# Sliding-block softmax by chained multiply-adds and ScalarE copies, with the buffers of the last chunks reassigned, in a two-part decode attention kernel

## Chip, cores, metric

One core of a Trainium2 chip. The metric is the time of one execution in device microseconds (us), median of several runs; lower is better. All runs told here are marked "fast" in the record: none lies more than 1.5% above the fastest of its kernel.

## The reference, cut to what matters

Two decode attentions over the same kind of cache, one query row per batch (4 batches), 32 query heads, head size 128; their outputs stand side by side.

```python
# A: 8 key heads, each for 4 query heads; only the last W = 2048 positions of 8192 ("sliding block")
scores = einsum("bhqd,bhkd->bhqk", q, k[:, :, Sk - W:]) * Dh ** -0.5
o_A = einsum("bhqk,bhkd->bhqd", softmax(scores), v[:, :, Sk - W:])   # then @ wo
# B: 32 key heads, all 8192 positions
o_B = einsum("bhqk,bhkd->bhqd", softmax(einsum("bhqd,bhkd->bhqk", q, k) * Dh ** -0.5), v)
out = concatenate([o_A @ wo_A, o_B @ wo_B], -1)
```

All inputs are bf16. The keys and values alone are 34 MB for A and 537 MB for B, each read once.

## The kernel before

The work is cut into 72 chunks: 0 to 7 are A (one key head, all four batches, 2 MB of keys and 2 MB of values), 8 to 71 are B (two heads of one batch, 4 MB and 4 MB). For each chunk PE transposes the keys (`tr`), VectorE or ScalarE copies them out of PSUM (`kt`), PE multiplies them with the queries (`sc`), the softmax follows, and one chunk later PE multiplies the probabilities (`pba` in A, `pbb` in B) with the values (`po`). All loads go through one queue, in program order, into ten buffers of 2 MB; each load waits for the last reader of its buffers.

In A a tile of 128 rows holds all four batches, so every score tile has 16 columns (4 batches x 4 heads), of which a row needs the four of its own batch. The kernel before multiplies with a mask and adds up, half a chunk at a time; GpSimd spreads the probabilities again to 16 columns.

```python
# buffers: at = first buffer of a load, take() returns what its last user must have done
at = HALF_A[kind][c % 5] if ch["ab"] == 0 else (0 if kind == "k" else 4) + 2 * (c % 2)
if kind == "v" and c == NC - 1:
    at = 8
waits = take((kind, c), at, 1 if ch["ab"] == 0 else 2, ("T", ch["s_last"]) if kind == "k" else ("pv", c))
...                                             # load order: k0 k1 v0 k2 v1 ... k69 v68 k70 k71 v69 v70 v71
def scores_out(c, half):                        # A only, twice per chunk
    dve.tensor_tensor(out=sel, in0=sc[:, half, :], in1=mk (broadcast), op=mult)      # 128x512
    dve.tensor_reduce(out=sA[half], in_=sel (b innermost), op=add)                   # 128x128
...                                             # stats_exp(c), A branch
    act.activation(ev, sA[:, c % 2, :], Exp)                                         # 128x256
    pool.tensor_tensor(out=pba, in0=ev (broadcast over b), in1=mkb (broadcast), op=mult)   # 128x1024
    dve.tensor_reduce(out=rs4, in_=ev, op=add)
    dve.tensor_tensor(out=rst, in0=rs4 (broadcast), in1=mk, op=mult)                 # 128x16
...                                             # end of the program
values_part(69, 71); values_only(70); emit_fin(69); emit_wos(71); norm_sum(71); values_only(71); emit_fin(71)
```

(The calls are shortened; the order and the operands are the kernel's.)

## Time and profile before

| | kernel before |
|---|---|
| time, median of 6 runs (lowest to highest) | 1388.06 us (1386.57 to 1389.91) |
| profiled run: span | 1384.0 us |
| DMA loads, share of 16 engines | 99.4% |
| busy PE, DVE (VectorE), ACT (ScalarE), POOL (GpSimd) | 1168.8, 672.5, 422.9, 19.2 us |
| mean granted clock of PE (share of full speed) | 0.932 |

PE's busy time is that of pipelined matmuls and says little by itself; the row to read first is that of the DMA engines. A transfer here is split over 16 DMA engines, each of which adds one to the semaphore when its share is in. The trace keeps the times of these 16 increments. "First" and "last landing" below are the first and the sixteenth.

### The profile page before, as it was taken

The page shows a single profiled execution, that of the slowest core. Times are in us where ns is not written, and L with a number is a line of the kernel's source. Part 1 is how long each engine was busy: PE and PEld are TensorE (multiplying, and loading weights), DVE is VectorE, ACT ScalarE, POOL GpSimd, SP SyncE. Part 2 cuts the span into 40 slices and gives each one's busy share as a digit, 9 for nine tenths or more (in the row PEclk, how much of TensorE's full clock was granted, in tenths as well). Part 3 has the DMA queues.
Part 4 walks back from the last instruction along what each step waited for, and adds up shares of the span by engine and source line. Part 5 has one row for each costly group of instructions (what it writes and reads, how often), then busy time and mean ns, then how long its engine had stood idle before and what let it go on. Part 6 is the DMA issues. An engine that isn't in the chain of part 4 may idle for free.

```text
span 1384.0 us, 57015 instructions
## 1 busy us (share of the span) xinstructions
PE 1168.8 (84%) x26768; PEld 1125.1 (81%) x26768; DVE 672.5 (49%) x1327; ACT 422.9 (31%) x617; POOL 19.2 (1%) x22
## 2 busy tenths in 40 slices
PE   4878868998889888888898889888888798888988
PEld 4767868897889788888888888887888788878887
DVE  2877534554445444444454444444444354444443
ACT  1333323332233223332233223322332233223332
POOL 1111000000000000000000000000000000000000
PEclk9999989999999899999999999999999999999998
DMA  9999999999999999999999999999999999999997
GB/s 398 416 416 423 425 428 421 417 428 434 430 433 430 428 431 434 429 428 432 430 434 430 429 431 433 431 427 432 429 435 429 431 430 433 431 429 430 430 409 319
DMA packets 29992, 588.02 MB, mean 425 GB/s; under 512 B 2656, under 2 KB 10864, under 8 KB 11120
## 3 DMA queue, kind: packets, MB, share of 16 engines
q1 hardware_dynamic: 29912, 587.22, 99.4%
q8 instruction: 40, 0.66, 0.2%
q14 instruction: 16, 0.13, 0.0%
q10 hardware_dynamic: 24, 0.01, 0.0%
HBM read 587.21 MB, written 0.01 MB: 424 GB/s over the span
## 4 chain that ended last, share of the span: by engine, by line
DMA 58%; PE 35%; DVE 5%; issue 2%; ACT 0%; SPq 0%; DVEq 0%
DMA kv<-in_B_k_cache_dram 55%; PE tr L322 21%; PE sc L324 9%; PE po L324 3%; DMA kv<-in_A_k_cache_dram 2%; DVE kt L385 1%; DVE sA L434 1%; DVE rsa L502 1%; PE ms L324 1%; DVE sel L427 1%; DVE rm L444 0%; DVE sA L491 0%; DVE rs L500 0%; ACT eA L494 0%; PE fin L324 0%
## 5 line engine op out<-in xcount | busy, mean ns | idle before, releaser
L322 PE MATMUL tr<-identb,kv 128*128 128x128 bf16 x8704 | 700.0, 231 | 159.6 <-DMA kv<-in_B_k_cache_dram 147.7
L385 DVE COPY kt<-tr 128x1024 bf16<-128x1024 bf16 x736 | 502.4, 690 | 468.8 <-PE tr L322 464.3
L322 PEld LDWEIGHTS tr<-identb,kv 128*128 128x128 bf16 x8704 | 555.7, 104 | 186.5 <-issue 98.2
L383 ACT ACTIVATE kt<-tr 128x1024 bf16<-128x1024 bf16 x352 | 360.2, 1023 | 646.4 <-PE tr L322 643.7
L324 PE MATMUL sc<-qb,kt 128*128 128x64 bf16 x8192 | 421.3, 196 | 2.5 <-DVE kt L385 2.2
L324 PEld LDWEIGHTS sc<-qb,kt 128*128 128x128 bf16 x8192 | 347.9, 100 | 5.4 <-DVE kt L385 2.6
L324 PE MATMUL po<-pbb,kv 128*128 128x64 bf16 (+1 forms) x8192 | 291.8, 192 | 14.9 <-issue 14.6
L324 PEld LDWEIGHTS po<-pbb,kv 128*128 128x128 bf16 x8192 | 264.5, 97 | 15.1 <-issue 12.9
L483 ACT ACTIVATE pbb<-sc,negb 64x128 bf16<-64x128 f32 x128 | 51.1, 399 | 296.4 <-DVE negb L473 288.5
L449 DVE TENSOR_REDUCE rm<-sc 64x1 f32<-64x128 f32 x128 | 37.0, 289 | 93.5 <-PE sc L324 92.6
L324 PE MATMUL sc<-qs,kt 128*128 128x64 bf16 (+3 forms) x512 | 25.9, 195 | 17.0 <-DVE kt L385 17.0
L473 DVE COPY negb<-ms 128x1 f32<-128x1 f32 (+1 forms) x72 | 11.4, 158 | 57.6 <-PE ms L324 57.6
L324 PEld LDWEIGHTS sc<-qs,kt 128*128 128x128 bf16 x512 | 20.7, 100 | 20.3 <-DVE kt L385 20.3
L461 DVE TENSOR_REDUCE gm<-ms 1x2 f32<-1x128 f32 (+1 forms) x72 | 20.1, 279 | 31.1 <-PE ms L322 30.8
L324 PE MATMUL ms<-identf,gx 1*128 1x1 f32 (+1 forms) x144 | 27.4, 257 | 0.6 <-DVE gx L465 0.6
L324 PEld LDWEIGHTS ms<-identf,gx 1*128 1x128 f32 (+1 forms) x144 | 21.3, 184 | 4.8 <-DVE gx L465 0.8
L483 ACT ACTIVATION_READ_ACCUMULATOR pbb<-sc,negb 64x1 f32 x128 | 23.7, 185 | 0.0
L324 PE MATMUL fin<-wos,oz 128*4 128x512 bf16 x64 | 20.1, 396 | 0.3 <-DVE oz L543 0.3
L322 PE MATMUL ms<-identf,rm 128*1 128x128 f32 (+1 forms) x72 | 19.6, 273 | 0.2 <-DVE rm L449 0.2
L324 PE MATMUL po<-pba,kv 128*128 128x64 bf16 x512 | 18.8, 193 | 0.0
L434 DVE TENSOR_REDUCE sA<-sel 128x128 f32<-128x512 f32 x16 | 17.0, 1063 | 0.5
L465 DVE TENSOR_SCALAR gx<-gm 1x128 f32<-1x128 f32 (+1 forms) x72 | 16.0, 222 | 2.5
(46 smaller groups left out, 179.8 us busy)
## 6 DMA issues: line engine op xcount, KB each, us to landing
kv<-in_B_k_cache_dram SPq DMA_DIRECT2D x64, 4096.0 KB, 26.9
kv<-in_B_v_cache_dram SPq DMA_DIRECT2D x63, 4096.0 KB, 31.5
kv<-in_A_k_cache_dram SPq DMA_DIRECT2D x8, 2048.0 KB, 27.6
kv<-in_A_v_cache_dram SPq DMA_DIRECT2D x8, 2048.0 KB, 26.5
kv<-in_A_wq_dram SPq DMA_DIRECT2D x1, 4096.0 KB, 12.6
kv<-in_B_wq_dram SPq DMA_DIRECT2D x1, 4096.0 KB, 27.7
wor<-in_A_wo_dram SPq DMA_DIRECT2D x8, 512.0 KB, 22.9
wor<-in_B_wo_dram SPq DMA_DIRECT2D x8, 512.0 KB, 32.4
```

The lines of the kernel that those rows point to most:

```text
L322: emit = lambda e: e.transpose(o, l, r)
L324: emit = lambda e: e.matmul(o, l, r, start=start, stop=stop)
L383: sch.add("act", lambda e: e.activation(dst, src, ACTF.Copy), waits=waits, key=("ev", s))
L385: sch.add("dve", lambda e: e.tensor_copy(dst, src), waits=waits, key=("ev", s))
L427: sch.add("dve", lambda e: e.tensor_tensor(out=sel[:, :].rearrange("p (j b c) -> p j b c", b=NB, c=REP), in0=sc[:, half, :].rearrange("p ( ...
L434: sch.add("dve", lambda e: e.tensor_reduce(out=dst, in_=sel[:, :].rearrange("p (j b c) -> p j c b", b=NB, c=REP), axis=AX.X, op=ALU.add), ...
L449: sch.add("dve", lambda e, src=src, pp=pp: e.tensor_reduce(out=rm[pp, m, 0:1], in_=src, axis=AX.X, op=ALU.max), waits=[("S", ch["s_last"]) ...
L461: sch.add("dve", lambda e: e.tensor_reduce(out=gm[0:C, m, 0:U], in_=src, axis=AX.X, op=ALU.max), waits=[("trm", c)], key=("gmax", c))
L465: sch.add("dve", lambda e: e.tensor_scalar(out=dst, in0=gv, scalar1=-scale, scalar2=None, op0=ALU.mult), waits=[("gmax", c)], key=("gx", c))
L473: sch.add("dve", lambda e: e.tensor_copy(negb[:, m, 0:C], ms[:, col:col + C]), waits=[("bc", c)], key=("negb", c))
L483: sch.add("act", lambda e, src=src, pp=pp, n=n, u=u: e.activation(pbv[pp, :, u], src, ACTF.Exp, bias=negb[pp, m, 0:1], scale=scale, accum_ ...
L502: sch.add("dve", lambda e: e.tensor_tensor(out=rst[0][:, m, :].rearrange("p (b c) -> p b c", b=NB), in0=bcast(rs4[:, m, :], [[0, NB], [1, ...
```

## The change

Its intent: in A, take the own-batch scores straight from PSUM by four chained operations with the mask column as a scalar, without a mask product and a reduction; let ScalarE write the probabilities, so that GpSimd is idle (a small VectorE product beside its product takes 1514 ns); at the end, use buffers that come free sooner, so that the keys of 70 and 71 and the values of 69 are issued earlier; and put small work of the end between matmuls.

```diff
-            if kind == "v" and c == NC - 1:
-                at = 8
+            at = {("k", NC - 2): 8, ("k", NC - 1): 0, ("v", NC - 1): 2}.get((kind, c), at)
...
-        def scores_out(c, half):
-            ... mask product over 512 columns, then reduction, for each half
+        def scores_out(c):
+            t = sA[:, c % 2, :].rearrange("p (j c) -> p j c", c=REP)
+            for b in range(NB):
+                src = sc[:, :, :].rearrange("p h (j x) -> p (h j) x", x=NB * REP)[:, :, b * REP:(b + 1) * REP]
+                waits = [("S", chunks[c]["s_last"]), "mk"] + ([("exp1", c - 2)] if c >= 2 else []) if b == 0 else [("own", c, b - 1)]
+                if b == 0:
+                    emit = lambda e, src=src: e.tensor_scalar(out=t, in0=src, scalar1=mk[:, 0:1], scalar2=None, op0=ALU.mult)
+                else:
+                    emit = lambda e, src=src, b=b: e.scalar_tensor_tensor(out=t, in0=src, scalar=mk[:, b:b + 1], in1=t, op0=ALU.mult, op1=ALU.add)
+                sch.add("dve", emit, waits=waits, key=("own", c, b))
...
-            sch.add("pool", lambda e: e.tensor_tensor(out=..., in0=bcast(ev, ...), in1=bcast(mkb[:, :], ...), op=ALU.mult), ...)
+            for b in range(NB):
+                sch.add("act", lambda e, b=b: e.activation(
+                    pbv.rearrange("p j (b c) -> p j b c", b=NB)[:, :, b, :], ev.rearrange("p (j c) -> p j c", c=C),
+                    ACTF.Copy, scale=mk[:, b:b + 1]), ...)
...
-        emit_fin(NC - 3)
-        emit_wos(NC - 1)
-        norm_sum(NC - 1)
-        values_only(NC - 1, NC)
+        values_only(NC - 2, {4: lambda: emit_fin(NC - 3), 8: lambda: emit_wos(NC - 1), 10: lambda: norm_sum(NC - 1)})
+        values_only(NC - 1, {})
```

(The call that worked on the first half in mid-chunk is gone as well, and so are the tiles `sel` and `mkb`.)

## The prediction

> **What bounds the kernel now.** I read the page first: parts 2 and 3 say how much of the span the DMA engines are busy, part 4 which engine the end was waiting for.
>
> ```profile
> span 1384.0 us, 57015 instructions
> DMA  9999999999999999999999999999999999999997
> GB/s 398 416 416 423 425 428 421 417 428 434 430 433 430 428 431 434 429 428 432 430 434 430 429 431 433 431 427 432 429 435 429 431 430 433 431 429 430 430 409 319
> q1 hardware_dynamic: 29912, 587.22, 99.4%
> DMA 58%; PE 35%; DVE 5%; issue 2%; ACT 0%; SPq 0%; DVEq 0%
> ```
>
> The 16 DMA engines are full from the first slice to the last but one; the loads alone take 99.4% of their time. The keys and values have to be read once (587 MB), so with an unchanged rate only the start and the last slice are left to win: 0.6% of 1384 is 8 us. The rate is a little lower in the first tenth (398 to 416 GB/s, the sliding-block part A) than later (about 430). The group list shows nothing else there that competes with DMA; the output weights, half a megabyte in 1 KB rows, come once per chunk in A and once per eight chunks in B, and I take the lower rate as their price. The change doesn't touch it.
>
> Next, the table by stretch, for the place where part A lies (about 8 to 132 us; columns: length, busy PE, weight load, DVE, ACT, POOL, clock, DMA share, GB/s).
>
> ```profile
> 8.00:132.00 124.00, 93.23 (x1967) 82.72 (x1968) 84.00 (x147) 39.14 (x43) 15.14 (x8) 0.96 1.02 420
> 300.00:1330.00 1030.00, 885.46 (x20314) 860.02 (x20311) 481.54 (x966) 314.78 (x470) 0.00 (x0) 0.93 1.00 431
> ```
>
> DMA share 1.02 in part A: although PE, DVE and ACT all wait there now and then, the loads don't. The DMA issues in order of time say the same: one issue of A's keys blocks for 18.02 us on a full queue at 18.9 us.
>
> Last, the end, from the chain of waits and from the issues of the DMA queue (start, length, what).
>
> ```profile
> 1295.94 0.33 SPq L292 DMA_DIRECT2D kv<-in_B_k_cache_dram  x1
> 1300.92 0.33 SPq L292 DMA_DIRECT2D kv<-in_B_v_cache_dram  x1
> 1312.34 22.22 SPq L292 DMA_DIRECT2D kv<-in_B_k_cache_dram  x2
> 1334.60 4.93 SPq L292 DMA_DIRECT2D kv<-in_B_v_cache_dram  x2
> 1339.57 1.94 SPq L289 DMA_DIRECT2D kv<-in_B_v_cache_dram  x4
> ```
> ```profile
> 1312.34 28.05 DMA kv<-in_B_k_cache_dram
> 1340.39 0.05 issue
> 1340.43 1.51 PE tr L322 x24
> ...
> 1366.78 1.98 issue
> 1368.76 1.08 PE po L324 x31
> ...
> 1377.01 3.23 PE po L324 x128
> ```
>
> The chunks are numbered 0 to 71. The keys of chunk 70 are issued at 1312.34, those of 71 only at about 1334 (22 us later, after the transposes of 69), and the values of 69, which stand behind them in the queue, at 1334.60. In that hole the one-microsecond table shows the DMA share at 0.53, 0.76 and 0.31 in three slices after 1332; over 1330 to 1342 it averages 0.875, so 1.5 us of DMA time are lost. This is what the new buffers aim at. From the landing of the keys of 70, at 1340.4, PE works nearly without a gap to the end.
>
> **What the Trainium skill says.** "DMA: Bandwidth & Descriptors", section "Why a DMA increments its semaphore by 16 and not by 1": a transfer is spread over up to 16 engines that finish independently, and the semaphore counts them. The trace agrees, and this decides the case: the 16 increments for the keys of 70 arrive from 1332.5 to 1340.4. Some engines are 7.9 us ahead of the slowest. The last increments of the successive 4 MB loads come at 1321.0, 1330.7, 1340.4, 1350.1, 1359.8 and 1369.5, always 9.7 us apart: the slowest engine lost nothing in the hole, and only engines that were ahead stood still. "SBUF — State Buffer", section "SBUF: two separate sides", puts the DMA side at 436 GB/s at most and 432 measured; 4.19 MB in 9.7 us is 432. The same section says that DVE and GpSimd share a port pair that one instruction holds to its end. The trace agrees: the 16-element product of row sums and mask, beside a POOL product, takes 1514 ns, while the 16-element product that writes the normalised outputs takes 165. "Runtime: NRT & Kernel Launch", "Instruction fetch mechanics": instructions come in 16 KiB blocks of 256; the trace has 40 such packets in the instruction queue.
>
> **The change part by part.** The costs of the operations touched, from the list of groups (mean ns after the busy time):
>
> ```profile
> L434 DVE TENSOR_REDUCE sA<-sel 128x128 f32<-128x512 f32 x16 | 17.0, 1063 | 0.5
> L496 POOL TENSOR_TENSOR pba<-eA,mkb 128x1024 bf16<-128x1024 bf16 x8 | 15.1, 1892 | 108.0 <-ACT eA L494 108.0
> L502 DVE TENSOR_TENSOR rsa<-rs,mk 128x16 f32<-128x16 f32 x8 | 12.1, 1514 | 0.3
> L427 DVE TENSOR_TENSOR sel<-sc,mk 128x512 f32<-128x512 f32 x16 | 10.9, 684 | 9.0 <-PE sc L324 8.9
> L491 DVE SCALAR_TENSOR_TENSOR sA<-sA,negb 128x256 f32<-128x256 f32 x8 | 3.4, 424 | 0.3
> L494 ACT ACTIVATE eA<-sA 128x256 bf16<-128x256 f32 x8 | 3.3, 416 | 4.3 <-DVE sA L491 4.3
> ```
>
> (1) Scores. Removed per A chunk: 2 x (684 + 1063) = 3.49 us of DVE. Added: 4 operations over 256 elements; the shift of the same size takes 424 ns, and I choose 450 for the PSUM source and the chained wait: 1.8 us. Net 1.7 us less per chunk, 13.5 us in the eight. The half that ran in mid-chunk moves to the end, where 1.75 us of work are replaced by 1.8, so the wait at the chunk's end stays.
>
> (2) Copies. POOL loses 1.89 us per chunk; ACT gains 4 x about 416 ns = 1.7 us. ACT is busy 39 of 124 us in A, so it becomes about 53. Without the POOL product, the product of row sums should fall from 1514 to about 170 ns: another 1.3 us of DVE per chunk, 10.8 us in all. A's chunks, now 12.15 us apart (between POOL products), may draw together to near the DMA's own pace, which I estimate at 4.72 MB / 415 GB/s = 11.4 us.
>
> Both lie beside a full DMA queue: DVE drops by some 24 us in total, and I count 0 us of it on the end.
>
> (3) Buffers. The keys of 70 go into slots free since part A and need no wait, so they are issued right after the values of 68, near 1301 instead of 1312; the keys of 71 wait for the transposes of 68 (about 1312), the values of 69 follow near 1317. The hole closes: 1.5 us of average DMA time. On the slowest engine, which had no hole, it is worth 0. The values of 70 and 71 are still issued at about 1339, and the landing at 1340.4 doesn't move.
>
> (4) Order at the end. Two output matmuls, the weight copy and the sum of 71 move into the values of 70. PE does the same matmuls in the same queue (0.53 + 0.32 us), and the DVE work was already under the values of 71. Gain 0. At most 0.5 us is there: the last values land at 1379.3; 16 matmuls of 26 ns after that would end at 1379.7, and PE ended at 1380.2.
>
> Sum: 0 from (1), (2); 0 from (3); 0 to 0.5 from (4). A little for jitter around the fetch stalls and engines that get ahead: 0.7 us off 1387.9, so 1387.2.
>
> **Rivals.** (a) The DMA hole is real time: the engines ahead help the slow one, or the queue is no longer short, and the end comes 1.5 to 3 us earlier, 1385 to 1386.4. For it: the 0.31 slice. Against: the even 9.7 us steps through the hole. (b) A slower part A delays the loads: ACT holds its evictions behind four copies, or both score banks are released later, so PE releases key buffers later. A 1 us delay per chunk would be 8 us, 1396, if it reached the DMA queue; but that is 20 to 30 us deep (median landing 26.5 to 31.5 us), and DVE gets 3 us per chunk back. (c) Part A's faster DVE is worth its 24 us: 1364. Only if the end followed DVE; it has 5% of the chain. (d) PE's tail changes: instruction fetch stalled PE 1.98 us at 1366.78, and after it the granted clock fell to 0.5, so that the values of 70 took 5.2 us. The stream changes by a few waits only; a different alignment could remove up to these 2 us, but then the last landing allows only 0.5, or add 2 us: 1389.5.
>
> **Range and chances.** The three runs before spread over 2.4 us. With (a) and (d) on either side, 1384.5 to 1389.8. Faster by 2% would be 28 us, more than three times what the DMA engines have idle; slower by 2% needs a stall of the queue that no view hints at. 0.01, 0.98, 0.01.
>
> **What would show it.** Right: DMA busy 99% or more as before; DVE about 24 us less, POOL about 4 us, ACT about 13 us more; no dip after 1330; the steps of last landings still 9.7 us, and the keys of 70 landing within 1.5 us of 1340; PE still unbroken from there to the end. Wrong, if the last landing of the values of 71 comes more than 1.5 us before 1379, if the DMA share in part A falls under 1, or if PE waits in the tail for values.

## The result, and the profile after

The changed kernel takes 1387.3 us, median of six runs (1384.51 to 1390.44), against 1388.06 us before. The ratio is 0.9994, with a 95% interval of 0.9977 to 1.0012: no difference that can be told from noise. Here and below a ratio is the mean time of one kernel's fast runs over that of the other's of the same rounds, so it is not quite the ratio of the medians quoted. The one profiled run of the changed kernel was its slowest of the six (1390.44), that of the kernel before (1385.85) was faster than all six of its timed runs; the spans of the two profiles, 1388.5 and 1384.0, therefore differ the wrong way round, and the tail below is where they do.

The page of the changed kernel, the lines that answer to those of before:

```profile
span 1388.5 us, 57012 instructions
...
DMA  9999999999999999999999999999999999999995
...
q1 hardware_dynamic: 29912, 587.22, 99.0%
...
DMA 60%; PE 36%; issue 2%; DVE 1%; ACT 0%; SPq 0%; ACTq 0%; DVEq 0%
```

The DMA engines are as full as before. In the chain that ended last, VectorE went from 5% to 1%, and DMA and PE took its place: much less of the chain runs through part A's softmax, yet the end didn't move.

The groups of the new operations, from the list with shapes kept apart (busy us, mean ns, then idle time before them):

```profile
L492 ACT ACTIVATE pba<-eA,mk 128x256 bf16<-128x256 bf16 x32 | 13.6, 497 | 0.3
...
L429 DVE SCALAR_TENSOR_TENSOR sA<-sc,mk,sA 128x256 f32<-128x256 f32 x24 | 11.6, 484 | 0.9
...
L427 DVE TENSOR_SCALAR sA<-sc,mk 128x256 f32<-128x256 f32 x8 | 3.9, 484 | 16.3 <-PE sc L322 16.2
...
L498 DVE TENSOR_TENSOR rsa<-rs,mk 128x16 f32<-128x16 f32 x8 | 1.4, 175 | 0.3
```

Four score operations at 484 ns instead of 3.49 us of products and reductions, and the small product of row sums at 175 ns instead of 1514 now that no GpSimd product runs beside it. DVE is busy 649.2 us (23.3 less), ACT 435.9 (13.0 more), POOL 4.1 (15.1 less). Part A's exponentials, 12.15 us apart before, come 11.09 us apart for as long as PE is not waiting for keys (at 50.73, 61.82, 72.91 and 84.00 us).

What became of that is in PE's waits between 84 and 132 us (total, times, longest), the end of part A. Before:

```profile
PE sc L324 <- DVE kt L385: 9.7, 11, 1.4
```

After:

```profile
PE tr L320 <- DMA kv<-in_B_k_cache_dram: 5.4, 1, 5.4
PE tr L320 <- DMA kv<-in_A_k_cache_dram: 2.7, 2, 2.4
PE sc L322 <- DVE kt L382: 1.1, 1, 1.1
```

8.6 us of waits for VectorE became 8.1 us of waits for loads. The largest is the one for the keys of chunk 8, the first of B. PE's transposes of them, in order of time, before and after:

```profile
120.36 1.50 PE L322 MATMUL tr<-identb,kv 128*128 128x128 bf16 x24
```
```profile
119.69 2.74 PE L320 MATMUL tr<-identb,kv 128*128 128x128 bf16 x24 [5.38 <-DMA kv<-in_B_k_cache_dram]
```

These keys land last at 119.7 us before and 119.6 after. The kernel before arrived 0.7 us later than its data; the changed kernel arrives 5.4 us earlier, waits, and starts at the same time (with its granted clock at 0.50 in 119.7 to 122.5: 24 transposes take 2.74 us instead of 1.50). Most of what part A gained is given back in this wait, and the rest two chunks on. The keys of chunk 10 land last at 158.2 in both profiles; PE waits for them in both, and starts at the same time:

```profile
158.29 0.40 PE L322 MATMUL tr<-identb,kv 128*128 128x128 bf16 x4 [1.44 <-DMA kv<-in_B_k_cache_dram]
```
```profile
158.23 2.74 PE L320 MATMUL tr<-identb,kv 128*128 128x128 bf16 x24 [2.81 <-DMA kv<-in_B_k_cache_dram]
```

At the end, the DMA issues of the changed kernel:

```profile
1299.96 0.33 SPq L290 DMA_DIRECT2D kv<-in_B_v_cache_dram  x1
1300.33 12.54 SPq L290 DMA_DIRECT2D kv<-in_B_k_cache_dram  x2
1317.52 21.53 SPq L290 DMA_DIRECT2D kv<-in_B_v_cache_dram  x2
1339.09 1.86 SPq L287 DMA_DIRECT2D kv<-in_B_v_cache_dram  x4
```

and the stretch 1330 to 1342 us (length, busy PE, weight load, DVE, ACT, POOL, clock, DMA share, GB/s), before and after:

```profile
1330.00:1342.00 12.00, 10.74 (x284) 10.48 (x281) 5.74 (x13) 3.46 (x8) 0.00 (x0) 1.00 0.88 355
```
```profile
1330.00:1342.00 12.00, 10.03 (x261) 9.84 (x259) 5.19 (x13) 2.97 (x7) 0.00 (x0) 0.98 1.00 431
```

The keys of 70 are issued at 1300.3 instead of 1312.3, the values of 69 at 1317.5 instead of 1334.6, and the hole is gone: 431 GB/s instead of 355. But the last landings stay where they were:

| first to last landing, us | before | after |
|---|---|---|
| keys 70 | 1332.5 to 1340.4 | 1332.4 to 1340.6 |
| keys 71 | 1345.8 to 1350.1 | 1342.1 to 1350.3 |
| values 69 | 1355.5 to 1359.8 | 1351.8 to 1360.0 |
| values 70 | 1365.3 to 1369.5 | 1361.6 to 1369.8 |
| values 71, last piece | 1375.2 to 1379.3 | 1371.5 to 1379.6 |

The engines that were ahead finish 3.7 us earlier. PE waits for the slowest one, and that one is as late as ever.

Last, the chain of waits at the end of the changed kernel (start, length, what):

```profile
1300.33 40.27 DMA kv<-in_B_k_cache_dram
1340.65 2.02 PE tr L320 x24
...
1358.98 2.02 issue
...
1372.53 1.14 issue
```

From the last landing of the keys of 70 to the end it is 1388.5 - 1340.6 = 47.9 us in this profile and 1384.0 - 1340.4 = 43.6 in that of before. The difference is in stops for which the profile names no waiting ("issue": 3.2 us against 2.0) and in matmuls at half clock, not in a change of work. The experiments give more such tails to compare.

### The profile page after: what moved, and what is told of

It is laid out like the page before. It is cut to its first block, busy times and chain, and to the rows that moved or that the text cites. A ratio compares the mean times of both kernels' runs of the same rounds, so it can differ in the third digit from the quotient of the medians.

```text
span 1388.5 us, 57012 instructions
## 1 busy us (share of the span) xinstructions
PE 1174.8 (85%) x26768; PEld 1132.3 (82%) x26768; DVE 649.2 (47%) x1326; ACT 435.9 (31%) x649; POOL 4.1 (0%) x14
## 4 chain that ended last, share of the span: by engine, by line
DMA 60%; PE 36%; issue 2%; DVE 1%; ACT 0%; SPq 0%; ACTq 0%; DVEq 0%
DMA kv<-in_B_k_cache_dram 58%; PE tr L320 21%; PE sc L322 9%; PE po L322 3%; DMA kv<-in_B_wq_dram 2%; PE fin L322 2%; PE ms L322 1%; DVE sA L429 1%; DVE kt L382 0%; DVE rm L438 0%; DVE sA L427 0%; ACT kt L380 0%; PE ms L320 0%; ACT pba L492 0%; DVE outsb L569 0%
## 5 line engine op out<-in xcount | busy, mean ns | idle before, releaser
L322 PEld LDWEIGHTS po<-pba,kv 128*128 128x128 bf16 x512 | 16.5, 98 | 0.0
```

The costliest lines, as they stand in the source:

```text
L322: emit = lambda e: e.matmul(o, l, r, start=start, stop=stop)
```

## The experiments

Twelve kernels were run, each against the kernel before in the same rounds. "Theory" is what the prediction rests on: the slowest DMA engine, then PE's tail, set the end.

**1. The softmax alone.** The changed kernel with the buffers and the order at the end put back (the two hunks of the diff that begin with `at =` and `values_only` undone).

> Kernel before with the new sliding-block softmax alone (four chained multiply-adds, ScalarE copies), old buffers and old order at the end. Main theory (the end is set by the slowest DMA engine, then by PE's tail): 0, time within 1 us of before, ratio 0.9993 to 1.0007; part A's chunks about 11.1 us apart as in the changed kernel, keys of chunk 70 still land last at 1340 to 1341 us, hole near 1332 us still there. Rival (parts of opposite sign cancel in the changed kernel): part A alone gains 2 us or more, ratio 0.9985 or less.

Ratio 0.9996 (0.9979 to 1.0013). The keys of 70 land last at 1339.4, the hole is there (DMA share 0.91 in 1330 to 1342), and PE waits 6.3 us for the keys of chunk 8. No gain of the softmax by itself is seen. The interval reaches down to 0.9979 (2.9 us), so the time alone doesn't exclude the rival's 2 us; neither this run nor run 2 shows parts of opposite sign.

**2. The buffers alone.** The kernel before with one line changed:

```diff
-            if kind == "v" and c == NC - 1:
-                at = 8
+            at = {("k", NC - 2): 8, ("k", NC - 1): 0, ("v", NC - 1): 2}.get((kind, c), at)
```

> Kernel before with only the buffers of the last chunks reassigned. Main theory: the hole in the DMA share after 1330 us closes (share 0.97 or more in 1330 to 1342), the first of the 16 increments of the late loads comes some 3 us earlier, but the last ones stay at 1340.5, 1350, 1360, 1369.5, 1379.5, so the time moves by less than 1 us. Rival (the hole is real time): 1.5 to 3 us faster, ratio 0.999 to 0.998.

Ratio 0.9994 (0.9977 to 1.0012). The DMA share in 1330 to 1342 is 1.00. The first landing of the keys of 71 comes at 1338.7 and the last at 1348.9, 10.1 us apart. The landings agree with the theory: from the last landing of the keys of 69, which the edit doesn't reach, to that of the keys of 70 it is 19.4 us in both kernels. The interval reaches down to 0.9977 (3.2 us), so the time alone excludes nothing of the rival's range.

**3 and 4. The hole made wider, behind and ahead of the keys of 70.** Two assignments of the same buffers. In the first the keys of 71, in the second those of 70, wait for the values of 68 to be used.

```diff
-            if kind == "v" and c == NC - 1:
-                at = 8
+            at = {("k", NC - 1): 4, ("v", NC - 2): 2, ("v", NC - 1): 8}.get((kind, c), at)     # behind
+            at = {("k", NC - 2): 4, ("v", NC - 2): 0, ("v", NC - 1): 8}.get((kind, c), at)     # ahead
```

> Kernel before with a wider hole behind the keys of 70: the keys of 71 take the buffer of the values of 68 (free near 1339 us), the values of 70 that of the keys of 69. The engines that are ahead now stand still from about 1332.5 to 1341, some 6 us on average instead of 1.5. Main theory (only the slowest engine counts, and it has its share of the keys of 70 to read until 1340.4): 0 to 1 us slower, and the 16 increments of the keys of 71 close up to within about 2 us, last near 1351. Rival (average DMA time counts): 4 to 5 us slower, ratio 1.003 or more.

> The same width of wait, placed where it meets the slowest engine: the keys of 70 take the buffer of the values of 68 (free near 1339 us), so they are issued near 1339 instead of 1312, after every engine has run dry at 1330.7. Main theory: the keys of 70 land last near 1351 instead of 1340.4 and the whole end follows, 9 to 11 us slower, ratio 1.0065 to 1.008. Rival (the last part of the program is not tied to this landing): under 5 us slower.

Behind: ratio 1.0014 (0.9999 to 1.0029), 1.9 us. Ahead: 1.0080 (1.0065 to 1.0094), 11.1 us. The stretch 1332 to 1342 with the hole behind, for which the kernel before has a DMA share of 0.86:

```profile
1332.00:1342.00 10.00, 8.09 (x216) 7.89 (x214) 3.92 (x11) 2.04 (x6) 0.00 (x0) 0.98 0.47 167
```

So the engines were idle for 5.3 of 10 us on average, 3.9 more than before, and the time rose by about half of that. The landings say how much the slowest engine lost: the keys of 71 came at 1350.4 to 1352.5, closed up as expected, last 2.4 us later than before and not 0 to 1. The keys of 71 were issued at 1338.77. Their landings less the 9.7 us step put the start of their data at 1340.7 to 1342.8 (an estimate), after the slowest engine had run dry at 1340.6; I had not allowed for that. Ahead of the keys of 70 the issue stands at 1337.34, all 16 increments come between 1349.1 and 1349.6, 9.2 us later than before, and the end follows. The expectation calls the two holes the same width, and they are not: in 1318 to 1342 the DMA share is 0.38 in run 4, 0.77 in run 3 and 0.94 before, so run 4 has 13.4 us more mean idling than the kernel before. A cost by mean idling would not be far from its 11.1 us either. What separates the two readings is run 3 alone: 3.9 us of mean idling, 2.4 us later last landings, 1.9 us of time, with the rival's 1.003 just above the interval (and no cost at all just inside it). Both came out some 1 us above or at the upper end of what was expected (1.9 against 0 to 1, 11.1 against 9 to 11).

**5. Half of one load left out** (chunk 40, values). Its output is wrong, which doesn't matter for the time.

```diff
+            if kind == "v" and c == 40:
+                src, dst = src[:, :8192], dst[:, :8192]
```

> Kernel before with half of one value load left out (2.1 of 4.2 MB, chunk 40, in mid-run; result wrong on purpose). Main theory (the DMA engines are the bound of the whole stretch before the tail): 4.9 us faster (half of the 9.7 us step), 3.9 to 5.9, ratio 0.9958 to 0.9972, and the keys of 70 land last near 1335.6. Rival (PE or its fetches pace the loop): under 2 us faster.

Ratio 0.9962 (0.9945 to 0.9979), 5.3 us for 2.1 MB; the keys of 70 land last at 1336.2, 4.2 us earlier. In mid-run the loads are the bound.

**6 and 7. The chain of score operations run twice, and five times, in part A.** Same result, more work for VectorE. The edit to the changed kernel, with n = 2 or 5:

```diff
-            for b in range(NB):
+            for i in range(n * NB):
+                b = i % NB
```

> Changed kernel with the chain of four score operations run twice per sliding chunk (same result, 4 x 484 ns = 1.94 us more DVE work per chunk, 15.5 us in all). Main theory (part A has slack against the DMA queue): no change, ratio 0.999 to 1.001; part A's chunks go from 11.1 to 12 or 13 us apart. Rival (part A is on the path): 8 to 15 us slower.

> Changed kernel with the chain run five times per sliding chunk (7.7 us more DVE work per chunk, 62 us in all). Main theory: slack ends. Chunks of A about 18.8 us apart against 11.4 us of loads, so PE falls some 55 to 60 us behind; the buffers let the loads run some 20 to 25 us ahead, so 25 to 45 us slower (ratio 1.018 to 1.032). Rival that part A's compute is hidden whatever it costs: under 5 us.

Both expectations fell. Twice: ratio 1.0140 (1.0122 to 1.0158), 19 us slower for 15.5 us of VectorE work. Five times: 1.0489 (1.0468 to 1.0510), 68 us. Part A has no slack against being slower. Its exponentials came some 14.9 us apart instead of 11.09, 3.8 us more for 1.94 us of work: the chain stands at the chunk's end, PE waits up to 3.8 us behind it, and its granted clock is lower in this stretch (0.66 to 0.94 in the 10 us slices from 50 to 110, against 1.0 before).

**8. The old order at the end.** The changed kernel with the output matmuls of 69, the weight copy and the sum of 71 back between the values of 70 and of 71.

> Changed kernel with the old order at the end (output matmuls of 69, weight copy and sum of 71 between the values of 70 and of 71). Main theory: PE does the same work, so 0, ratio 0.999 to 1.001. Rival (interleaving saves or costs the 0.85 us of these matmuls): 0.6 to 1 us either way, ratio 0.9993 or 1.0007 and clear of noise.

Ratio 1.0005 (0.9990 to 1.0021). This is against the kernel before; the changed kernel, from which it differs in the order alone, was not in these rounds. No effect is seen; the interval doesn't exclude 1 us.

**9 and 10. The last loads in halves.** If PE's tail begins with the last landing of the keys of 70, it can begin sooner with half of them. In run 9 the keys of 70 and 71, in run 10 the values of 69 and 70 too, are two transfers with a semaphore each, and PE waits for each half where it needs it.

```diff
+            if kind == "k" and c >= NC - 2:
+                for h in range(2):
+                    x = slice(h * 8192, (h + 1) * 8192)
+                    sch.add_dma("sp", ... dst[:, x], src[:, x] ..., key=("kl", c, h * 8))
+                return
...
-                    waits = [("k", c), "c_identb"] if g == 0 else []
+                    waits = [("k", c), "c_identb"] if g == 0 and c < NC - 2 else []
+                    waits += [("kl", c, g)] if ("kl", c, g) in sch.tk else []
```

> Changed kernel with the keys of chunks 70 and 71 loaded in two halves each, so that PE can start on the first half of the keys of 70. Main theory as the traces have refined it (end = last landing of the keys of 70, near 1340, plus a tail of PE of 43.6 to 48.7 us that instruction-fetch stalls and half clock lengthen; floor = last landing of the values of 71, near 1379, plus about 4 us): the tail starts some 4.8 us earlier and its stalls fall beside the loads, 2 to 4 us faster than before, ratio 0.997 to 0.9985. Rival (the DMA engines alone set the end): within 0.7 us.

> The same, and the values of 69 and 70 in two halves as well, so that PE is not left to turn cold while it waits for a whole load. Main theory: as the run with keys in two, or up to 1.5 us better; 2.5 to 4.5 us faster than before, ratio 0.9968 to 0.9982, end within 5 us of the last landing. Rival: within 0.7 us.

Run 9: 1385.77 us, ratio 0.9979 (0.9966 to 0.9993), 2.9 us. Run 10: 1386.29 us, 0.9986 (0.9972 to 0.9999), 2 us, a little less than expected. In run 9 the halves of the keys of 70 land last at 1336.1 and 1341.0, and the tail, from 1336.1 on, still has stops of 2.0, 0.5, 2.0 and 0.9 us in its chain; they now fall beside the loads. In run 10 the end hangs on the very last piece of the values:

```profile
1340.09 38.78 DMA kv<-in_B_v_cache_dram
1378.87 0.05 issue
```

The span is 1383.3, 4.4 us after that landing at 1378.9. This is the floor of the design as it stands: the last landing plus 16 matmuls, the output matmuls, a copy and the store. Both runs contain the change. Against the changed kernel they were not measured in the same rounds, so what the halves add to it is likely and not shown.

**11. Six operations instead of four.** After runs 6 and 7 I looked for the margin at the issue of the keys of chunk 10 and put it at some 9 us. A smaller dose was to test that: the changed kernel with the batches taken as 0, 1, 0, 1, 2, 3.

> Changed kernel with six score operations per sliding chunk instead of four (0.97 us more DVE work each, half of what the chain run twice adds). From the runs so far the margin is at one place, the issue of the keys of 10: before at 135.2 us, with the slowest engine supplied until 146.9, so some 9 us. Chain twice came at 154.7 and lost 10 there. Theory: chunks about 13 us apart (half of the 3.8 us that chain twice added), issue near 142 to 145 us, inside the margin or just at it: 0 to 2 us slower, ratio 0.999 to 1.0015. Rival (each us of DVE in part A counts in full, so that there is no margin): 8 us slower, ratio 1.006.

Ratio 1.0053 (1.0039 to 1.0067), 7.4 us: my margin is refuted too, and the rival's 8 us was nearly right. The keys of chunk 10 did come as expected (issued at 144.0, landed last at 158.1, as before), so they are not the place. PE is late before that, at chunk 8. PE's transposes of that chunk's keys in this run:

```profile
127.29 1.50 PE L320 MATMUL tr<-identb,kv 128*128 128x128 bf16 x24
```

PE starts chunk 8 at 127.29, 6.9 us later than in the kernel before, with no wait, and from the keys of chunk 17 on (first landing 299.5 against 292.4) to those of 70 (1339.6 against 1332.5) the engines that are ahead are 7.1 us late. The last landing, which is what PE waits for, is 4.4 us late at the keys of 17 (301.5 against 297.1) and 7.7 at those of 70 (1348.1 against 1340.4). With the chain twice PE starts chunk 8 16.7 us late; the keys of 70 land first 16.9 and last 17.2 us late. In between, from 135 to 250 us, PE is at work nearly all the time and stops now and then with no wait named (up to 7.7 us at once before, 6.1 here), so it doesn't catch up (in the kernel before its one wait for keys there is the 1.4 us at chunk 10). The front of the loads is short of free buffers there: in the kernel before two steps of first landings, near 250 and 270 us, are 11.7 and 11.0 us instead of 9.7.

**12. The keys of chunk 8 in two halves as well.** If PE's start of chunk 8 decides, the way to let the faster softmax out is to have chunk 8 earlier.

> Changed kernel with the keys of chunks 8 (the first of the full attention), 70 and 71 in two halves each. Refined theory: what the new softmax gains in part A is given back where PE waits for the keys of chunk 8 (5.4 us in the changed kernel, last landing 119.6; the kernel before comes 0.7 us after them), and from there to about 250 us PE has no slack, so lateness at this point counts in full (6.9 us late with two more operations cost 7, 16.7 us late with the chain twice cost 17 to 18) and earliness needs the keys earlier. With the first half landing near 115, PE starts chunk 8 some 4.5 us sooner, the keys of 14 and 15 are issued some 4 us earlier, and the hole of the engines that are ahead near 250 (2 to 3 us) shrinks. In the time: 0 to 2.5 us beyond the run with the keys of 70 and 71 in two, so ratio 0.996 to 0.998. Rival (that wait is as free as all else in part A): keys of 14 and 15 issued as before and ratio as the run with the keys in two, 0.998.

```profile
114.95 1.51 PE L328 MATMUL tr<-identb,kv 128*128 128x128 bf16 x24 [1.57 <-DMA kv<-in_B_k_cache_dram]
```

PE starts chunk 8 at 114.95 instead of 119.69, and the keys of 14 and 15 are issued at 215.4 and 237.6 instead of 219.6 and 241.1. The first landings then step by 9.7 us without a gap from 230 to 289 us. All this was expected, but it doesn't show the mechanism. At chunk 10 the head start is gone:

```profile
158.43 2.42 PE L328 MATMUL tr<-identb,kv 128*128 128x128 bf16 x24 [2.69 <-DMA kv<-in_B_k_cache_dram]
```

PE starts it on the landing of its keys, as the kernels before and after do. And profiles without this edit show the same issues and steps: run 2, whose part A is that of the kernel before, has the keys of 14 and 15 issued at 215.3 and 236.5, and run 8, with that of the changed kernel, at 216.6 and 237.9, both with steps of at most 10.3 us up to 289. So whether the front has a gap near 250 us differs from profile to profile by itself. The time is 1384.72 us, ratio 0.9978 (0.9966 to 0.9990), the same as run 9: as the rival had it, starting chunk 8 earlier adds nothing that can be seen. (Where the gap is closed, the engines that are ahead land earlier: first landing of the keys of 18 at 309.5 instead of 313.4 in the changed kernel, last at 318.0 and 318.2.) Its runs lie within 1.5 us (1384.53 to 1385.98), those of the kernel before in the same rounds within 4.8. It is clear of the kernel before; it was never run in the same rounds as the changed kernel (1387.3), so a gain over that one is likely and not shown.

## Why the prediction was right, point by point

- **The bound.** Right. Half a load less took 5.3 us off where 4.9 were worked out from the 9.7 us step.
- **The hole is worth 0 on the slowest engine.** Right, and shown by the landings: it closed, and the last landings stayed within 0.4 us. A hole with nearly four times the idling (5.3 us against 1.4) behind the slowest engine cost 1.9 us, half of what mean idling would give. This holds for a hole some 50 us before the end. For one early in the run the profiles suggest otherwise: from the keys of 21 to those of 69 the first landing takes 941.3 to 941.5 us in every profile but run 5's, the last one 943.2 to 947.9, and the longer the closer the two were at 21 (7.9 us apart in run 2: 943.7; 4.7 before: 944.7; 2.0 in run 11: 947.9). So it seems that time which the leading engines lose near 250 us reaches the slowest one in part before the end; no run tested that, and why is open.
- **Costs of the operations.** The terms were near: 484 ns for a score operation (450 assumed), 497 for a copy (416 assumed), 175 for the product freed of GpSimd (170); DVE 23.3 us less (24), ACT 13.0 more (13), POOL 15.1 less (15).
- **Part A counts 0.** The sum was right; one step of its reasoning failed. The prediction put A's work "beside a full DMA queue" and set against rival (b) that the queue is "20 to 30 us deep (median landing 26.5 to 31.5 us)". A deep queue is not slack for PE. Runs 6, 7 and 11 show that A could not have become slower by even 1 us per chunk unpunished: PE met the keys of chunk 8 to within 0.7 us, and after that it had only 1.4 us of reserve (the wait for the keys of chunk 10) until 250 us. The figure that rival (b) gave for a delay that did reach the queue, 8 us and 1396, is what run 11 measured with a delay of that size (1396.17). The gain, in turn, ends in the waits for the keys of chunks 8 and 10, which I had not named; that these make it 0 is read from the traces, and by time a gain of up to 2.9 us is not excluded (run 1).
- **The order at the end: 0 to 0.5 us.** No effect was seen. But the statement that PE works "nearly without a gap" from 1340.4 and that only 0.5 us is to be had rested on one profile with a short tail, 43.6 us. Counted the same way, from the last landing of the keys of 70 to the end, the changed kernel and runs 1, 2, 3, 4 and 8 have 47.9, 47.3, 48.7, 46.5, 46.4 and 45.6 us. The floor was some 2 to 3 us away, as runs 9, 10 and 12 show. One sign that the prediction had set for being right, PE unbroken from 1340 to the end, did not come: the changed kernel has stops of 2.0 and 1.1 us there.
- **The number.** 1387.2 was forecast and 1387.3 measured. That they agree to 0.1 us is luck: the median of the kernel before came out at 1387.7 to 1388.7 in other rounds. (The 587 MB that the prediction calls keys and values are all loads; keys and values are 571 of them.)
- **Rival (a)** fell with the landings of the changed kernel and of run 2 and with the time of run 3, **rival (c)**, 24 us, with the result and run 1. **Rival (d)**, other stops of PE in the tail, is seen: 0.5 to 2.3 us each, one to four to a profile. Whether they make the scatter of the times (1384.5 to 1390.4 in six runs of the changed kernel) is not shown, with one profile per kernel. What these stops are was read, not tested: each begins 0.4 to 2.1 us after the start of a packet of 16 KB in the instruction queue (at 1366.25 for the stop at 1366.78 before, at 1358.45 for that at 1358.98 after). One thing speaks for the packets: from 300 to 1330 us, where PE runs one loop of its program (`emit_looped`), the kernel before has none of them, and PE waits for keys alone (144.5 us in 52 waits) and never stops without a named wait.

## What to carry to other kernels

When loads bound a kernel, ask of every hole in the DMA share which engine stood still: only the last of the sixteen landings releases the consumer. Near the end a hole among the others cost little here; early in the run, the profiles suggest, it is not free. A stage that hides behind a full queue can be worth nothing when made faster and cost in full when made slower; look for the point where it meets its data, and how near they meet, before calling it slack. And where the end hangs on the landing of one large transfer, splitting that transfer is a smaller change than all the work around it.

## What the Trainium skill lacked or had wrong

- "DMA: Bandwidth & Descriptors" says that the engines of one transfer finish independently, but gives no time for how far apart: here 7.9 us for the keys of 70 before and 10.1 us for the keys of 71 in run 2, about one whole step of 9.7 us; nor what a hole costs in which only the engines that are ahead stand still (in run 3, 3.9 us more mean idling cost 1.9 us).
- "Runtime: NRT & Kernel Launch", section "Instruction fetch mechanics", calls the crossing of a 16 KiB boundary mostly hidden. Here the fetch packets took 0.9 to 1.4 us, and PE stopped for 0.5 to 2.3 us at one to four of them in each tail, and for 7.7 us once near 200 us in the kernel before (from 199.08; the packet there begins only at 203.92). That the fetch is the cause is a reading of the trace; no run tested it.
